# RWKV attention and squared-ReLU FFN on one core: small steps placed by a list scheduler, fixed tiles and PSUM banks, and DMA transposes for 16 of 24 chunks

## The chip, the cores and the metric

The kernel runs on one NeuronCore of a Trainium2 chip. The time is device microseconds from start to end of the program; lower is better. The profile's span (first to last instruction) is about 2 us shorter than the time. Engines: PE is TensorE (PEld its weight loads), DVE is VectorE, ACT is ScalarE, POOL is GpSimd, SP is SyncE, which here only issues DMAs. In the traces here each engine works its instructions off in program order, so one that waits holds up all those behind it: PE stood still for 9.0 us before one transpose (below).

## The reference

Two stages. A recurrent attention with decay `w` and a bonus `u`, then an FFN `relu(x W1)^2 W2`.

```python
batch, n_heads, seq, head_dim = 4, 8, 768, 48          # r, k, v
n_tokens, d_model, d_ff = 3072, 384, 2048
for t in range(S):
    cur = einsum('bhd,bhe->bhde', u * k[t], v[t])
    y[t] = einsum('bhd,bhde->bhe', r[t], state + cur)
    state = w * state + einsum('bhd,bhe->bhde', k[t], v[t])
x = y as (3072, 384)
h = maximum(x @ w_in, 0)
out = (h * h) @ w_out                                   # float32
```

## The kernel before

The sequence is cut into 24 chunks (6 pieces of 128 steps, 4 batches). Within a chunk the recurrence becomes matmuls. Each chunk passes these steps (their names return below):

- kh and rt: k and r times powers of w, to bf16 (POOL; DVE for the first two chunks). P0: r times k times u (POOL), summed by `du` and multiplied with v to `dv` (DVE).
- T: eight 128x128 transposes of kh and rt on PE, copied out of PSUM by ACT (rkT). A: eight matmuls; Bm: two masks on DVE. Y and U: the chunk's output and state update. xs: Y plus dv (DVE). X: three transposes of xs on PE, copied by ACT into xT.
- For each pair of chunks, F1: the first layer in eight slices of six matmuls, relu on ACT, square on DVE; F2: the second layer, eight slices of four matmuls, then a copy by ACT and a store.

The order is written by hand: eight slots per period, in each slot a slice of F1 of one pair, of F2 of the pair before, and a piece of attention of the pair after.

```python
psT, psA, psY, psU: one buffer each (psA has 2 banks);  psH: bufs=2;  psO: bufs=1   # all 8 PSUM banks
...
def piece_F1(g, s):
    hp = psH.tile([128, 2, GT], FP32, tag="H")
    ...                                        # 6 matmuls
    nc.scalar.activation(hr, hp, AF.Relu)
    nc.vector.tensor_mul(hq, hr, hr)           # square, SBUF to SBUF, bf16
...
prep(0, nc.vector); prep_du(0, nc.gpsimd); prep(1, nc.vector); prep_du(1, nc.gpsimd)
for s in range(NS): load_w1(s)                 # 8 DMAs issued by POOL
for s in range(NS): load_w2(s)                 # 8 more
def period(ga, g1, g2):
    for s in range(8):
        if g1 is not None: piece_F1(g1, s)
        if g2 is not None: piece_F2(g2, s)
        if ga is not None:
            att(ga, s)                         # s=0: cast v, T, du/dv; 1: A, T; 2: A, du/dv; 3,4: Y, U; 5,6: X
            ...
            preps(ga + 1, s)                   # POOL, one pair ahead
```

Of the kernel before, what the change touches and what calls it, by code (L numbers as in the profile page):

```python
# [8 lines left out]
FP32 = mybir.dt.float32  # L10
BF16 = mybir.dt.bfloat16
AF = mybir.ActivationFunctionType
ALU = mybir.AluOpType


@with_exitstack
def kernel(
# [19 lines left out]
    HD = H * D  # L37
# [10 lines left out]
    loads = ctx.enter_context(tc.tile_pool(name="loads", bufs=7))  # L48
    work = ctx.enter_context(tc.tile_pool(name="work", bufs=3))
    hid = ctx.enter_context(tc.tile_pool(name="hid", bufs=3))  # L50

    psT = ctx.enter_context(tc.tile_pool(name="psT", bufs=1, space=bass.MemoryType.PSUM))
    psA = ctx.enter_context(tc.tile_pool(name="psA", bufs=1, space=bass.MemoryType.PSUM))
    psY = ctx.enter_context(tc.tile_pool(name="psY", bufs=1, space=bass.MemoryType.PSUM))
    psU = ctx.enter_context(tc.tile_pool(name="psU", bufs=1, space=bass.MemoryType.PSUM))
    psH = ctx.enter_context(tc.tile_pool(name="psH", bufs=2, space=bass.MemoryType.PSUM))
    psO = ctx.enter_context(tc.tile_pool(name="psO", bufs=1, space=bass.MemoryType.PSUM))

    def bcast_rows(src):
        return bass.AP(  # L60
            tensor=src.tensor, offset=src.offset, ap=[[0, 128], list(src.ap[0]), list(src.ap[1])]
        )


    r_v = r.rearrange("b h (c t) d -> b c t h d", t=L)
    k_v = k.rearrange("b h (c t) d -> b c t h d", t=L)
    v_v = v.rearrange("b h (c t) d -> b c t h d", t=L)
    out_v = out.rearrange("(n t) o -> n t o", t=L)
    w_in_t = moe_w_in.rearrange("(c p) f -> p c f", p=128)
    w_out_t = moe_w_out.rearrange("(f p) o -> p f o", p=128)  # L70

    nat = {}

    def load(i):
        if i >= N:
            return
        c, b = i // B, i % B
        rf = loads.tile([128, H, D], FP32, name=f"rf_{i}", tag="rf")
        kf = loads.tile([128, H, D], FP32, name=f"kf_{i}", tag="kf")
        vf = loads.tile([128, H, D], FP32, name=f"vf_{i}", tag="vf")  # L80
        nc.sync.dma_start(out=rf, in_=r_v[b, c])
        nc.sync.dma_start(out=kf, in_=k_v[b, c])
        nc.sync.dma_start(out=vf, in_=v_v[b, c])  # L83
        nat[i] = (rf, kf, vf)

    W1, W2 = [], []

    def load_w1(s):
        t = const.tile([128, CCH, GT], BF16, name=f"W1_{s}")
        nc.gpsimd.dma_start(out=t, in_=w_in_t[:, :, GT * s : GT * (s + 1)])  # L90
        W1.append(t)

    def load_w2(s):
        t = const.tile([128, 2, d_model], BF16, name=f"W2_{s}")
        nc.gpsimd.dma_start(out=t, in_=w_out_t[:, 2 * s : 2 * s + 2, :])
        W2.append(t)
# [4 lines left out]
    nc.sync.dma_start(out=wb, in_=bcast_rows(w))  # L101
    load(0)
    ub = const.tile([128, H, D], FP32, name="ub")
    nc.sync.dma_start(out=ub, in_=bcast_rows(u))
    for i in range(1, 4):
        load(i)
    load(4)
    load(5)

# [4 lines left out]
    nc.gpsimd.iota(njcol_i, pattern=[[0, 1]], base=L - 1, channel_multiplier=-1)  # L114
    identity = const.tile([128, 128], BF16, name="identity")
# [16 lines left out]
    )  # L132

    tcol = const.tile([128, 1], FP32, name="tcol")
    nc.vector.tensor_copy(tcol, tcol_i)
    njcol = const.tile([128, 1], FP32, name="njcol")
    nc.vector.tensor_copy(njcol, njcol_i)
    NB = 4
    rt_buf, kh_buf = [], []
    for j in range(NB):  # L140
        tr = const.tile([128, H, DP], BF16, name=f"rt_{j}")
        tk = const.tile([128, H, DP], BF16, name=f"kh_{j}")
        nc.vector.memset(tr[:, :, D:DP], 0.0)
        nc.vector.memset(tk[:, :, D:DP], 0.0)
        rt_buf.append(tr)
        kh_buf.append(tk)
    wrow = const.tile([1, 2, HP, 128], FP32, name="wrow")
    nc.vector.memset(wrow, 0.0)
    esel = const.tile([1, 2, 2 * D], FP32, name="esel")
    nc.vector.memset(esel, 0.0)  # L150
    nc.vector.memset(esel[:, 0, 0:D], 1.0)
    nc.vector.memset(esel[:, 1, D : 2 * D], 1.0)

    logw = const.tile([128, H, D], FP32, name="logw")
    nc.scalar.activation(logw, wb, AF.Ln)
    Wkhat = const.tile([128, H, D], FP32, name="Wkhat")
    nc.scalar.activation(Wkhat, logw, AF.Exp, scale=njcol)
    Wt2 = const.tile([128, H, D], FP32, name="Wt2")
    nc.scalar.activation(Wt2, logw, AF.Exp, scale=tcol)
    logw_p = logw.rearrange("p (a e) d -> p e a d", e=2)  # L160
    for e in range(2):
        nc.scalar.activation(  # L162
            wrow[:, e, :, 64 * e : 64 * e + D], logw_p[0:1, e], AF.Exp, scale=float(L)
        )

    WLm = const.tile([128, HP, 2 * D], FP32, name="WLm")
    wl_ps = psU.tile([128, HP, 2 * D], FP32, name="wl_ps", tag="U", padded_shape=[None, None, 128])
    for hc in range(HP):
        for e in range(2):
            nc.tensor.matmul(  # L170
                wl_ps[:, hc, :],
                wrow[:, e, hc, :],
                esel[:, e, :],
                start=(e == 0),
                stop=(e == 1),
                skip_group_check=True,
            )
    nc.scalar.copy(WLm, wl_ps)

    S0W = [const.tile([128, HP, 2 * D], BF16, name=f"S0W_{b}") for b in range(B)]  # L180


    du_in, vbs, dvs, rkTs, Bms, xss, xTs = {}, {}, {}, {}, {}, {}, {}

    def prep(i, eng):
        rf, kf, vf = nat[i]
        eng.tensor_mul(kh_buf[i % NB][:, :, 0:D], kf, Wkhat)  # L187
        eng.tensor_mul(rt_buf[i % NB][:, :, 0:D], rf, Wt2)

    def prep_du(i, eng):  # L190
        rf, kf, vf = nat[i]
        P0 = work.tile([128, H, D], FP32, name=f"P0_{i}", tag="P0")
        eng.tensor_mul(P0, rf, kf)  # L193
        eng.tensor_mul(P0, P0, ub)  # L194
        du_in[i] = P0

    def cast_v(i):
        vb = work.tile([128, H, D], BF16, name=f"vb_{i}", tag="vb")
        nc.scalar.copy(vb, nat[i][2])
        vbs[i] = vb  # L200

    def bonus(i):
        P0 = du_in.pop(i)
        du = work.tile([128, H], FP32, name=f"du_{i}", tag="du")
        nc.vector.tensor_reduce(du, P0, axis=mybir.AxisListType.X, op=ALU.add)  # L205
        dv = work.tile([128, H, D], FP32, name=f"dv_{i}", tag="dv")
        du_b = bass.AP(
            tensor=du.tensor, offset=du.offset, ap=[list(du.ap[0]), list(du.ap[1]), [0, D]]
        )
        nc.vector.tensor_mul(dv, nat[i][2], du_b)  # L210
        dvs[i] = dv

    def piece_T(i):
        pt = psT.tile([128, 2, HP, 128], BF16, name=f"pt_{i}", tag="T")
        for j, src in ((1, kh_buf[i % NB]), (0, rt_buf[i % NB])):
            for hc in range(HP):
                nc.tensor.transpose(  # L217
                    pt[:, j, hc, :],
                    src[:, 2 * hc : 2 * hc + 2, :].rearrange("p a b -> p (a b)"),
                    identity,  # L220
                )
        rkT = work.tile([128, 2, HP, 128], BF16, name=f"rkT_{i}", tag="rkT")
        nc.scalar.copy(rkT, pt)  # L223
        rkTs[i] = rkT

    def piece_A(i):
        rkT = rkTs[i]
        Ap = psA.tile([128, 2, HP, 128], FP32, name=f"Ap_{i}", tag="A")
        Bm = work.tile([128, 2, HP, 128], BF16, name=f"Bm_{i}", tag="Bm")
        for hc in range(HP):  # L230
            for e in range(2):
                p0 = 64 * e
                nc.tensor.matmul(
                    Ap[:, e, hc, :],
                    rkT[p0 : p0 + D, 1, hc, :],
                    rkT[p0 : p0 + D, 0, hc, :],
                    start=True,
                    stop=True,
                    skip_group_check=True,
                )  # L240
        for e in range(2):
            nc.vector.tensor_mul(Bm[:, e], Ap[:, e], mask_b)
        Bms[i] = Bm

    def piece_YU(i):
        c, b = i // B, i % B
        rkT, Bm, vb = rkTs.pop(i), Bms.pop(i), vbs.pop(i)
        Y = psY.tile([128, HP, 2 * D], FP32, name=f"Y_{i}", tag="Y", padded_shape=[None, None, 128])
        for hc in range(HP):
            if c > 0:  # L250
                nc.tensor.matmul(
                    Y[:, hc, :], rkT[:, 0, hc, :], S0W[b][:, hc, :],
                    start=True, stop=False, skip_group_check=True,
                )
# [175 lines left out]
```

## Time and profile before

| | before |
|---|---|
| time, median of 3 runs | 221.29 us (220.57 to 221.61) |
| span of the profiled run | 219.5 us |
| PE, DVE, ACT, POOL busy | 81%, 70%, 53%, 60% of the span |

From the first page of the profile, the busy shares. Section 1 gives busy time; section 2 cuts the span in 40 slices of 5.5 us, a digit being the busy share in tenths.

```profile
PE 177.5 (81%) x1784; PEld 131.4 (60%) x1784; DVE 154.1 (70%) x254; ACT 115.8 (53%) x199; POOL 131.5 (60%) x134
PE   0854117587998998998989989989989879999973
DVE  3486006799979889699699798896996993753300
POOL 2597469995396594892993975947929980000000
DMA  5999999996129148075092190391750010010111
```

PE is poorly used in the first nine slices (0 to 49 us), where the DMA line reads 9 for most of the time, and nearly full afterwards. The table of busy time by window has the same in numbers (columns: stretch, its length, busy us and instruction count of PE, PEld, DVE, ACT and POOL, granted PE clock, share of DMA time, GB/s). The share adds up the times of all packets over 16 engines; it reads 1.20 in one stretch here, so it serves to compare stretches and is not a fraction of what the DMA could do:

```profile
0.00:21.30 21.30, 9.39 (x79) 7.71 (x80) 12.45 (x30) 7.71 (x13) 13.85 (x24) 1.00 0.96 168
21.30:49.30 28.00, 14.33 (x127) 9.90 (x127) 13.48 (x21) 9.07 (x16) 22.56 (x24) 1.00 1.20 185
49.30:185.00 135.70, 124.62 (x1335) 93.47 (x1333) 116.08 (x179) 82.99 (x143) 95.14 (x87) 1.00 0.42 92
```

What PE waits for in the first 50 us, from the table of waits (total us, times, longest):

```profile
PE pt_369 L217 <- POOL kh_153 L187: 9.0, 1, 9.0
PE wl_ps L170 <- ACT wrow L162: 6.4, 1, 6.4
```

PE waits 9.0 us for POOL to prepare chunk 2 (kh). POOL is late since it issues sixteen weight loads first, from 12.9 to 30.7 us; from the tenth on it waits 0.5 to 0.9 us before each one for an earlier weight load to land. The DMA view shows what the weight loads do to the loads of r, k and v (KB each, us from issue to landing): 4.4 us without them, 17.8 us beside them.

```profile
kf_91<-in_k_dram SPq DMA_DIRECT2D x1, 192.0 KB, 4.4
...
rf_122<-in_r_dram SPq DMA_DIRECT2D x1, 192.0 KB, 17.8
```

From 64 us on the chain of waits repeats every 15.13 us (63.62 to 78.75). One period of it (start, us, what):

```profile
63.62 0.60 ACT hr_0_841 L310
...
65.21 0.55 DVE du_863 L205
...
66.56 1.14 DVE hq_1_878 L312
67.69 1.20 DVE Bm_885 L242 x2
68.89 0.62 DVE hq_2_916 L312
...
72.49 0.48 DVE xs_979 L272
...
73.01 0.20 PE Y_1000 L251
...
78.06 0.67 PE hp_0_1099 L301 x6
78.75 0.60 ACT hr_0_1106 L310
```

The chain runs through relu, then eight microseconds of DVE in its program order, then Y on PE, then about six microseconds of PE in its program order, and relu again. The step from DVE to PE is the single buffer of Y: Y_1000 starts at 73.01 us, just after xs_979 has read the Y before it out of that buffer.

### The profile page before, as it was taken

Reading aid. Unit: us, or ns where it says so; the run is one execution under the profiler, and the core shown is the slowest. Engines: PE = TensorE matmul, PEld = TensorE weight load, DVE = VectorE, ACT = ScalarE, POOL = GpSimd, SP = SyncE. Lnnn points to the kernel's source line nnn. Section 1 sums busy time; section 2 is a strip of 40 time slices with the busy share of each in tenths; the row PEclk is TensorE's granted clock in tenths of the full one; section 3 lists DMA queues with packets and bytes.
Section 4 is the critical chain, followed back from the end, with each engine's and each line's share of the span. In section 5 each row is a group of like instructions: output and inputs, shape, how many; then the busy total and the mean of one; then the engine's idle time right before and its main releaser. Section 6 shows DMA issues by size and latency. Waiting matters only on the chain.

```text
span 219.5 us, 4540 instructions
## 1 busy us (share of the span) xinstructions
PE 177.5 (81%) x1784; PEld 131.4 (60%) x1784; DVE 154.1 (70%) x254; ACT 115.8 (53%) x199; POOL 131.5 (60%) x134
## 2 busy tenths in 40 slices
PE   0854117587998998998989989989989879999973
PEld 0733015375776776766767757767667657777741
DVE  3486006799979889699699798896996993753300
ACT  4341104466486476583764864765846737745520
POOL 2597469995396594892993975947929980000000
PEclk9999999999999999999999999999999999999999
DMA  5999999996129148075092190391750010010111
GB/s 113 194 186 178 174 182 185 184 200 131 37 56 200 39 104 172 14 162 129 1 214 75 50 206 36 73 184 37 157 130 3 36 39 36 0 39 36 39 52 56
DMA packets 84020, 22.70 MB, mean 103 GB/s; under 512 B 75552, under 2 KB 84000, under 8 KB 84000
## 3 DMA queue, kind: packets, MB, share of 16 engines
q1 hardware_dynamic: 78624, 19.27, 41.8%
q0 software_dynamic: 5376, 3.15, 9.8%
q8 instruction: 14, 0.23, 0.5%
q14 instruction: 6, 0.05, 0.1%
HBM read 20.84 MB, written 4.72 MB: 116 GB/s over the span
## 4 chain that ended last, share of the span: by engine, by line
PE 37%; DVE 34%; issue 8%; DMA 7%; POOL 6%; ACT 4%; SPq 2%; POOLq 0%; ACTq 0%
DMA W_6_211<-in_moe_w_in_dram 5%; DMA kf_99<-in_k_dram 2%; PE o_3289 L323 1%; PE o_3269 L323 1%; PE o_3216 L323 1%; PE o_3152 L323 1%; PE o_730 L323 1%; SPq L83 1%; PE o_3062 L323 1%; PE o_2055 L323 1%; PE o_1790 L323 1%; PE o_995 L323 1%; PE o_2830 L323 1%; PE o_2585 L323 1%; PE o_1260 L323 1%
## 5 line engine op out<-in xcount | busy, mean ns | idle before, releaser
L301 PEld LDWEIGHTS <-W_0_199 128*128 128x128 bf16 x72 | 7.3, 102 | 2.9 <-issue 0.7
L170 PE MATMUL wl_ps<-esel,wrow 1*128 1x96 f32 x16 | 3.7, 423 | 6.4 <-ACT wrow L162 6.4
L205 DVE TENSOR_REDUCE du_380<-P_2_291 128x8 f32<-128x384 f32 x1 | 0.6, 554 | 10.9 <-POOL P_2_291 L194 10.9
L217 PEld LDWEIGHTS <-kh_153 128*128 128x128 bf16 x24 | 1.9, 103 | 10.2 <-POOL kh_153 L187 9.5
L217 PE MATMUL pt_369<-identity,kh_153 128*128 128x128 bf16 x4 | 0.6, 307 | 9.0 <-POOL kh_153 L187 9.0
L301 PEld LDWEIGHTS <-W_3_205 128*128 128x128 bf16 x72 | 6.3, 100 | 2.1 <-issue 0.2
L301 PEld LDWEIGHTS <-W_1_201 128*128 128x128 bf16 x72 | 6.9, 102 | 0.9
L301 PEld LDWEIGHTS <-W_2_203 128*128 128x128 bf16 x72 | 6.9, 102 | 0.9
L170 PEld LDWEIGHTS wl_ps<-esel,wrow 1*128 1x128 f32 x16 | 3.5, 326 | 6.4 <-ACT wrow L162 6.4
L301 PEld LDWEIGHTS <-W_6_211 128*128 128x128 bf16 x72 | 6.6, 98 | 0.7
L301 PEld LDWEIGHTS <-W_7_213 128*128 128x128 bf16 x72 | 6.6, 98 | 0.7
L301 PEld LDWEIGHTS <-W_5_209 128*128 128x128 bf16 x72 | 6.4, 98 | 0.7
L301 PEld LDWEIGHTS <-W_4_207 128*128 128x128 bf16 x72 | 6.4, 97 | 0.7
L223 ACT COPY rkT_378<-pt_369 128x1024 bf16<-128x1024 bf16 x1 | 1.0, 1012 | 9.6 <-PE pt_369 L217 9.6
L280 POOL TENSOR_TENSOR S0W_185<-ts_716,WLm 128x384 bf16<-128x384 f32 x1 | 1.0, 1040 | 5.8 <-DVE ts_716 L279 5.8
L193 POOL TENSOR_TENSOR P_0_191<-rf_90,kf_91 128x384 f32<-128x384 f32 x1 | 1.4, 1372 | 4.1 <-DMA kf_91<-in_k_dram 4.1
L280 POOL TENSOR_TENSOR S0W_185<-ts_1776,WLm 128x384 bf16<-128x384 f32 x1 | 1.1, 1110 | 3.9 <-DVE ts_1776 L279 3.9
L280 POOL TENSOR_TENSOR S0W_187<-ts_981,WLm 128x384 bf16<-128x384 f32 x1 | 1.1, 1109 | 3.9 <-DVE ts_981 L279 3.9
L280 POOL TENSOR_TENSOR S0W_185<-ts_1246,WLm 128x384 bf16<-128x384 f32 x1 | 1.1, 1109 | 3.9 <-DVE ts_1246 L279 3.9
L280 POOL TENSOR_TENSOR S0W_187<-ts_1511,WLm 128x384 bf16<-128x384 f32 x1 | 1.1, 1109 | 3.9 <-DVE ts_1511 L279 3.9
L280 POOL TENSOR_TENSOR S0W_187<-ts_2041,WLm 128x384 bf16<-128x384 f32 x1 | 1.1, 1109 | 3.9 <-DVE ts_2041 L279 3.9
L280 POOL TENSOR_TENSOR S0W_185<-ts_2306,WLm 128x384 bf16<-128x384 f32 x1 | 1.1, 1109 | 3.9 <-DVE ts_2306 L279 3.9
(1198 smaller groups left out, 735.0 us busy)
## 6 DMA issues: line engine op xcount, KB each, us to landing
wb<-in_w_dram SPq DMA_DIRECT2D x1, 192.0 KB, 3.6
rf_90<-in_r_dram SPq DMA_DIRECT2D x1, 192.0 KB, 4.1
kf_91<-in_k_dram SPq DMA_DIRECT2D x1, 192.0 KB, 4.4
vf_92<-in_v_dram SPq DMA_DIRECT2D x1, 192.0 KB, 4.4
ub<-in_u_dram SPq DMA_DIRECT2D x1, 192.0 KB, 4.4
rf_98<-in_r_dram SPq DMA_DIRECT2D x1, 192.0 KB, 4.4
kf_99<-in_k_dram SPq DMA_DIRECT2D x1, 192.0 KB, 4.7
vf_100<-in_v_dram SPq DMA_DIRECT2D x1, 192.0 KB, 4.8
```

Source lines behind the costliest of these rows:

```text
L83: nc.sync.dma_start(out=vf, in_=v_v[b, c])
L170: nc.tensor.matmul(wl_ps[:, hc, :], wrow[:, e, hc, :], esel[:, e, :], start=(e == 0), stop=(e == 1), skip_group_check=True,)
L193: eng.tensor_mul(P0, rf, kf)
L205: nc.vector.tensor_reduce(du, P0, axis=mybir.AxisListType.X, op=ALU.add)
L217: nc.tensor.transpose(pt[:, j, hc, :], src[:, 2 * hc : 2 * hc + 2, :].rearrange("p a b -> p (a b)"), identity,)
L223: nc.scalar.copy(rkT, pt)
L280: nc.gpsimd.tensor_mul(S0W[b], ts, WLm)
L301: nc.tensor.matmul(hp[:, fi, :], W1[s][:, c, 128 * fi : 128 * (fi + 1)], xT[:, c, :], start=(c == 0), stop=(c == CCH - 1), skip_group_chec ...
L323: nc.tensor.matmul(ops[i], hsq[g, f // 2][:, f % 2, L * j : L * (j + 1)], W2[f // 2][:, f % 2, :], start=(f == 0), stop=(f == FCH - 1), sk ...
```

## The change

Intent: keep PE always supplied. The program is cut into some 900 small steps with a duration, an engine, what they depend on, and the buffers and banks they take and free. A list scheduler inside the kernel (it runs when the program is built) simulates the engines and two DMA queues and fixes the order and every buffer. Along with it:

- DMA transposes replace PE's T and X for chunks 8 to 23 (`nT=8, nX=8`);
- half of the squares go to ACT, the other half are taken on DVE as PSUM times relu;
- the weight loads wait (a "gate") until v of chunk 2 has landed; from chunk 2 on, r/k/v come for two chunks per DMA; weights in eight loads of double size;
- WLm (the decay table) is built by POOL instead of sixteen fp32 matmuls; kh/rt of chunks 0 to 7 go to DVE;
- PSUM: three banks shared by all attention steps, three for F1, two for F2.

The core of the diff, cut (`...`):

```diff
+class Step: ...
+def order_steps(steps, pools, sw_rate=0.75, hw_rate=0.17): ...
+PLAN = dict(per=6.2, loads=[...], nprep=8, p1set=2, nT=8, nX=8, gates=[('v', 2), ('v', 2)],
+            sq=(1, 3, 5, 7), ldlead=26, lead=-1, f1lag=0.5, f2lag=8, relup=-3, sqp=-2)
+POOLS = dict(ldr=2, ..., rkT=6, bank=3, bankH=3, bankO=2, Bm=3, xs=3, xT=2, hr=6, hq=28, os=3, ts=2)
...
-        nc.gpsimd.dma_start(out=t, in_=w_in_t[:, :, GT * s : GT * (s + 1)])
+        s_g = st(f"gate{part}", "POOL", 0.1, [Ld[x, i]], prio=-102, emit=go)
+            Ws.append(st(f"W{part}{s}", "POOL", 0.78, [s_g], prio=..., dma=2.32, emit=go))
...
+    def f_XB(i):
+            nc.sync.dma_start_transpose(out=rkTb[...], in_=rk[...].rearrange("p a h d -> p (a h d)"))
+    def f_xX(i):
+            nc.sync.dma_start_transpose(out=xTb[...][:, :, L * (i % 2) : L * (i % 2 + 1)], in_=xsb[...])
...
-        nc.vector.tensor_mul(hq, hr, hr)
+            if eng == "ACT":
+                nc.scalar.activation(hq, hr, AF.Square)
+            else:
+                nc.vector.tensor_mul(hq, hp, hr)        # hp is the PSUM bank
...
+    order, given = order_steps(steps, POOLS)
+    for s in order:
+        s.emit()
```

## The prediction

> **What bounds the kernel now**, by the table of busy time by window, the timeline and the chain of waits:
>
> - 0 to 49.3 us: start-up. PE is busy 23.7 us, 3.7 of them in fp32 matmuls for WLm. The DMA engines are full (168 to 185 GB/s). Sixteen weight loads, issued by POOL from 12.9 us, slow the r/k/v loads: landing takes 4.4 us before and up to 17.8 us beside them. POOL, issuing in order against a full ring, cannot prepare chunk 2 until 30.7 us; PE, in order too, waits 9.0 us for that (table of waits).
> - 49.3 to 185 us: a pattern with a period of 15.13 us per pair of chunks. From the timeline's starts, PE's work in it is: first layer 8 x 0.655, second layer 8 x 0.65, A 2 x 0.36, Y 2 x 0.37, U 2 x 0.17, transposes 2 x (0.44 + 0.17): 13.5 us. About 1.6 us are stalls, and the chain runs half of each period through DVE: masks (0.68 each, two per chunk) and squares, which take 0.42 us alone but 1.1 to 1.2 beside POOL's work.
> - After 185 us: nearly pure PE work, then 3.8 us of tail.
>
> **What the change does**
>
> 1. Transposes of 16 of 24 units leave PE: 1.22 us per pair. PE's work falls to 12.3 us per pair and about 152 us in all. Their copies (1.01 and 0.48 us per chunk) leave ACT.
> 2. Half of the squares go to ACT; the others read PSUM, and I estimate 0.69 us from the mask, equal in size and also from PSUM. DVE falls from 12.9 to about 10 us per pair; ACT stays near 9.2, POOL at 11.2. So PE remains the bound, with POOL close behind.
> 3. The order is finer; PSUM has three attention, three first-layer and two output banks: most of the 1.6 us should go. My period: 12.6 to 13 us.
> 4. Weights start only after the first four chunks' loads (near 18 us), so POOL and PE have work meanwhile; WLm's fp32 matmuls go. The first 45 us stay limited by DMA: the weights need about 25 us while sharing. I expect PE to idle about 21 us before it saturates.
> 5. Added: 32 DMA transposes, of 256 KB and 96 KB. No run shows their duration yet. The Trainium skill, "DMA: Bandwidth & Descriptors", section "Latency and other measured facts", gives 261 GB/s; my estimate from it is 1.0 and 0.4 us. Per pair the DMA then has loads 6.2, stores 1.1 and transposes 2.8: about 10 of 12.7 us.
>
> **Sum** (estimate): 152 PE work + 21 start-up idle + 4 stalls + 4 tail = 181 us; the measured time lies near the span (221.3 against 219.5). Predicted 181, range 171 to 196. Faster by over 2%: 0.96; within 2%: 0.02; slower: 0.02.
>
> **What would show it.** Step 1: PE's busy time down by over 10 us. Steps 2, 3: period near 12.7, PE above 95% busy from about 45 us on, DVE near 78%. Step 4: the first first-layer matmul near 22 us, without a 9 us PE wait after it. Step 5: transposes landing within 4 us, no PE wait on them.
>
> **What would make it wrong.** Transposes much slower than estimated, holding up loads and stores in the one SP queue; loads starving behind weights, so that the fixed PE order stalls at chunks 4 to 7; POOL slowed by DVE's port use to over 12.7 us per pair.

## The result, and the profile after

| | before | after |
|---|---|---|
| time, median | 221.26 us (4 runs) | 183.05 us (182.37 to 184.16, 4 runs) |
| ratio of fast runs | | 0.8285 (95%: 0.8252 to 0.8318) |
| span | 219.5 us | 180.6 us |
| PE, DVE, ACT, POOL busy | 81, 70, 53, 60% | 89, 71, 65, 59% |

Ratios here and below are the mean time of a kernel's fast runs over that of the kernel before in the same rounds, so not quite the ratio of the medians.

The page of the changed kernel, the same lines:

```profile
PE 160.6 (89%) x1592; PEld 118.2 (65%) x1592; DVE 128.6 (71%) x216; ACT 117.5 (65%) x214; POOL 106.8 (59%) x116
PE   0344769899999999999999999999999999999991
DVE  3399998997388838959979696778777889631310
POOL 2346998024940999599879977986968980000000
DMA  3999999999949649979799799897896255221102
```

From slice 9 on (a slice is 4.5 us here) PE is at 9 to the end. And DMA, which had been idle half of the time after 50 us, is now mostly at 7 to 9 tenths up to 140 us. By window:

```profile
0.00:22.00 22.00, 9.00 (x86) 5.84 (x86) 15.78 (x35) 9.08 (x15) 11.18 (x23) 1.00 0.94 180
22.00:45.00 23.00, 20.00 (x217) 16.00 (x216) 20.33 (x35) 16.37 (x29) 11.96 (x13) 1.00 1.23 194
100.00:120.00 20.00, 20.00 (x208) 14.43 (x206) 14.54 (x25) 13.58 (x26) 17.12 (x18) 1.00 0.94 182
```

What PE waits for in the whole run:

```profile
PE bank L429 <- DVE rk L382: 10.2, 4, 6.3
PE bank L454 <- ACT rkT L436: 2.2, 2, 1.1
PE bank L536 <- DVE xs L506: 1.9, 3, 0.8
```

L429 is T, L454 is A, L536 is X: all of them belong to the start. After 38 us the table of waits has 0.6 us in all. The new DMAs (x count, us to landing):

```profile
rkT<-rk SPq DMA_TRANSPOSE x16, 3.4
xT<-xs SPq DMA_TRANSPOSE x16, 3.8
```

**Where the time came from.** Busy PE is a poor measure of work, because matmuls overlap (an F1 matmul lasts 273 ns, yet the next one starts 109 ns after it) and run slower in the start-up (417 to 421 ns, 213 ns apart). How long they run slower differs too: the first record of a full clock is at 40.0 us in the kernel before, at 29.6 us in `before_gate` and at 28.2 us in the changed kernel, so a part of what counts below as lost in the start-up is PE running slower, and not standing still. I count instead the matmuls of each kind in a stretch and price them at their start-to-start times at full speed (F1 0.655 us per six, F2 0.65 per four, T 0.44 per eight, A 0.36, Y 0.37, U 0.17, X 0.17 per step). This is my own arithmetic on counts from the trace. `before_gate` and `before_three` are experiments explained below.

| useful PE work, us | before | before_gate | before_three | after |
|---|---|---|---|---|
| 0 to 49.3 us | 12.2 | 16.6 | 17.2 | 25.3 |
| 49.3 to 100 us | 44.8 | 44.6 | 47.1 | 49.6 |
| 100 to 140 us | 36.2 | 35.8 | 37.6 | 39.7 |
| whole run | 160.6 | 160.6 | 153.5 | 150.9 |
| span minus work | 58.9 | 54.1 | 47.7 | 29.7 |

So the span fell by 38.9 us: 9.7 us because PE has less to do, 29.2 us because it loses less time. Of these 29.2, 13.1 come from the first 49.3 us and 16.1 from later.

### The profile page after: what moved, and what is told of

It reads as the page before. It is cut to its first block, busy times and chain, and to the rows that moved or that the text cites. A ratio compares the mean times of both kernels' runs of the same rounds, so it can differ in the third digit from the quotient of the medians.

```text
span 180.6 us, 4082 instructions
## 1 busy us (share of the span) xinstructions
PE 160.6 (89%) x1592; PEld 118.2 (65%) x1592; DVE 128.6 (71%) x216; ACT 117.5 (65%) x214; POOL 106.8 (59%) x116
## 4 chain that ended last, share of the span: by engine, by line
PE 79%; DVE 9%; DMA 4%; ACT 2%; SPq 2%; issue 1%; DVEq 0%
PE bank L638 34%; PE bank L604 32%; PE bank L454 4%; PE bank L483 3%; DMA ub<-in_u_dram 2%; DMA xT<-xs 2%; PE bank L478 2%; PE bank L429 2%; DVE rk L382 2%; SPq L351 2%; DVE xs L506 2%; DVE dv L411 2%; PE bank L495 2%; DVE Bm L467 1%; ACT rkT L436 1%
## 5 line engine op out<-in xcount | busy, mean ns | idle before, releaser
L618 ACT ACTIVATE hr<-bank 128x512 bf16<-128x512 f32 x96 | 55.9, 595 | 29.4 <-PE bank L604 27.6
L604 PE MATMUL bank<-xT,W 128*128 128x256 bf16 x576 | 73.8, 273 | 0.4 <-DVE hq L629 0.3
L638 PE MATMUL bank<-W,hq 128*128 128x384 bf16 x384 | 72.0, 326 | 0.0
L604 PEld LDWEIGHTS <-W 128*128 128x128 bf16 x576 | 55.0, 98 | 11.8 <-issue 0.9
L638 PEld LDWEIGHTS <-hq 128*128 128x128 bf16 x384 | 36.1, 98 | 19.3
L629 DVE TENSOR_TENSOR hq<-bank,hr 128x512 bf16<-128x512 f32 x48 | 32.6, 683 | 17.4 <-ACT hr L618 17.4
L467 DVE TENSOR_TENSOR Bm<-bank,maskJT 128x512 bf16<-128x512 f32 x48 | 31.1, 681 | 8.2 <-PE bank L454 8.1
L388 POOL TENSOR_TENSOR P<-ldr,ldk 128x384 f32<-128x384 f32 x24 | 28.2, 1177 | 9.9 <-DMA ldr<-in_r_dram 9.9
L528 POOL TENSOR_TENSOR S0W<-ts,WLm 128x384 bf16<-128x384 f32 x16 | 16.5, 1031 | 29.1 <-DVE ts L522 28.9
L626 ACT ACTIVATE hq<-hr 128x512 bf16<-128x512 bf16 x48 | 30.2, 630 | 1.1
L397 POOL TENSOR_TENSOR P<-P,ub 128x384 f32<-128x384 f32 x22 | 22.9, 1043 | 1.4
L651 ACT COPY os<-bank 128x384 f32<-128x384 f32 x24 | 11.4, 476 | 12.4 <-PE bank L638 12.1
L429 PE MATMUL bank<-identity,rk 128*128 128x128 bf16 x64 | 7.5, 273 | 10.5 <-DVE rk L382 10.2
L382 POOL TENSOR_TENSOR rk<-ldr,Wt 128x384 bf16<-128x384 f32 x16 | 16.6, 1040 | 0.1
L429 PEld LDWEIGHTS <-rk 128*128 128x128 bf16 x64 | 5.5, 120 | 12.4 <-DVE rk L382 11.5
L454 PE MATMUL bank<-rkT 48*128 48x128 bf16 x192 | 10.6, 233 | 2.5 <-ACT rkT L436 2.2
L483 PE MATMUL bank<-vb,Bm 128*128 128x48 bf16 x192 | 12.2, 189 | 0.4 <-DVE Bm L467 0.4
```

What stands on the lines that cost most here:

```text
L382: e.tensor_mul(rk[slot[f"rk{i}"]][:, j, :, 0:D], ld[x][slot[f"{x}P{i // 2}"]][:, i % 2], tab)
L388: nc.gpsimd.tensor_mul(P0b[slot[f"P0{i}"]], ld["r"][slot[f"rP{i // 2}"]][:, i % 2], ld["k"][slot[f"kP{i // 2}"]][:, i % 2])
L397: (nc.vector if eng == "DVE" else nc.gpsimd).tensor_mul(t, t, ub)
L454: nc.tensor.matmul(heads(f"bA{i}{e}", "bank", 128)[:, hc, :], rkT[p0 : p0 + D, HP + hc, :], rkT[p0 : p0 + D, hc, :], start=True, stop=True ...
L467: nc.vector.tensor_mul(Bmb[slot[f"Bm{i}"]][:, e], heads(f"bA{i}{e}", "bank", 128), mask_b)
L483: nc.tensor.matmul(Y[:, hc, D * e : D * (e + 1)], Bm[:, e, hc, :], vb[:, 2 * hc + e, :], start=(c == 0), stop=True, skip_group_check=True,)
```

## The experiments

Twelve kernels, all with correct results. "before" in their ratios is the kernel before, run in the same rounds. In all_pe, sq_back, no_gate, banks_back and tuned the scheduler computes the order and the buffers anew, so these change along with the edit; xbar_twice, twice_split and warm keep the order.

### 1. All transposes back on PE (all_pe)

```diff
-nT=8, nX=8
+nT=24, nX=24
```

> The changed kernel with all 24 units transposed on TensorE again (nT=24, nX=24); the list scheduler reorders accordingly. Theory A (TensorE is saturated from about 38 us on, so its work adds one to one): 16 units x 0.61 us = 9.8 us more, 183 to 193 us (190 to 196), PE busy near 100% in 60 to 140 us as before, and 16 rkT copies (1.01 us) and 16 xT copies (0.48 us) back on ACT, 24 us in all, which still fit. Rival B (the gain is the order and the banks; the DMA transposes only move work to a DMA queue that is itself nearly full): at most 186 us.

Measured: 191.61 us (191.5 to 191.72), ratio 0.867. That is 8.6 us above the changed kernel; 9.8 were expected. Its PE work counts 160.8 us, and span minus work is 28.9 us, about the same as with DMA transposes (29.7). The two kernels over 80 to 140 us, first all_pe:

```profile
80.00:140.00 60.00, 60.00 (x661) 46.11 (x658) 46.25 (x74) 48.70 (x88) 48.98 (x48) 1.00 0.57 126
```

and the changed kernel:

```profile
80.00:140.00 60.00, 59.65 (x623) 44.47 (x620) 49.02 (x79) 42.60 (x79) 50.55 (x50) 1.00 0.92 189
```

PE is full in both. Theory A holds: with PE saturated, work taken off it counts nearly one to one. The price is on the DMA, whose share rises from 0.57 to 0.92.

### 2. Squares back on DVE (sq_back)

```diff
-sq=(1, 3, 5, 7)
+sq=()
-                nc.vector.tensor_mul(hq, hp, hr)
+                nc.vector.tensor_mul(hq, hr, hr)
```

> The changed kernel with all 96 squares on VectorE from SBUF as in the kernel before (hr*hr), nothing on ACT. Theory A: VectorE gets 48 squares more and each lasts 0.42 to 1.2 us beside POOL's work; its busy time goes from 129 us to about 180 us, so VectorE becomes the bound: 200 us (192 to 212). Rival B (VectorE had room, squares do not matter once the order is fine): at most 187 us.

Measured: 195.52 us (194.11 to 196.6), ratio 0.8842. Theory A holds. The 96 squares last 770 ns on average (683 ns for the 48 that read PSUM in the changed kernel). DVE is full from 60 to 100 us (39.3 of 40 us), but PE loses little there. The losses lie in 40 to 60 and 100 to 160 us: there the counted work of PE is 67.2 us of 80, against 78.7 in the changed kernel, and DVE is busy 75.3 us. One of these stretches, and PE's wait for DVE's masks over the whole run:

```profile
140.00:160.00 20.00, 18.10 (x184) 13.18 (x185) 19.96 (x31) 8.84 (x17) 15.81 (x15) 1.00 0.68 131
PE bank L454 <- DVE Bm L467: 3.8, 5, 2.2
```

Total DVE busy was 161 us, not 180: the squares were slowed less than I had taken from the kernel before. With this plan, the split of the squares is needed for PE to be the bound.

### 3. Weight loads without the gate (no_gate)

```diff
-        s_g = st(f"gate{part}", "POOL", 0.1, [Ld[x, i]], prio=-102, emit=go)
-            Ws.append(st(f"W{part}{s}", "POOL", 0.78, [s_g], ...
+            Ws.append(st(f"W{part}{s}", "POOL", 0.78, [], ...
```

> The changed kernel with the gate before the weight loads taken away, so that POOL issues all eight at about 2 us. Theory A (r/k/v loads starve beside weight loads): the loads of chunks 0 and 1 land only when the weights do (about 25 us), the first first-layer matmul comes after 35 us instead of 27.4 us, total 190 to 200 us. Rival B (the same bytes have to come in anyway, so only their order changes): 181 to 185 us.

Measured: 193.84 us (192.76 to 193.91), ratio 0.8759; the first F1 starts at 36.8 us instead of 27.5. The loads of v for chunks 0 and 1 took 14.3 us to land, against 4.5 us:

```profile
ldv<-in_v_dram SPq DMA_DIRECT2D x2, 192.0 KB, 14.3
```

The same bytes in another order cost 10.8 us. Theory A holds.

### 4. The kernel before with the squares split (before_sq)

```diff
-        nc.vector.tensor_mul(hq, hr, hr)
+        if s % 2:
+            nc.scalar.activation(hq, hr, AF.Square)
+        else:
+            nc.vector.tensor_mul(hq, hp, hr)
```

> The kernel before with one part of the change: odd squares on ACT, even ones on VectorE reading PSUM. Theory A (half of each 15.13 us period runs through VectorE, squares being the stretched part): the period falls towards TensorE's 13.5 us, to about 14.1 us; some 10 periods, so 221 to about 211 us (206 to 216). Rival B (the stalls come from the coarse order and the single banks, not from the squares): over 218 us.

Measured: 218.41 us (217.59 to 218.91), ratio 0.9878. Theory A fell. DVE went down to 47.8 of 80 us (60 to 140 us), yet the period only went from 15.13 to 14.59 us (79.86 to 94.45 in its chain). The chain now runs through ACT, where relu, square and the rkT copy stand in one order, and then as before through DVE and PE. Relieving the engine in the chain did not free PE; the loop closed through the next one.

### 5. The kernel before with later weight loads (before_gate)

```diff
-    for s in range(NS): load_w1(s)
-    for s in range(NS): load_w2(s)
 ...
                 preps(ga + 1, s)
+                if ga == 0 and s == 7:
+                    for t in range(NS): load_w1(t)
+                    for t in range(NS): load_w2(t)
```

> The kernel before with only the weight loads issued later: POOL issues the sixteen after it has prepared chunks 2 and 3 (about 22 us instead of 12.9 us). Theory A (weights crowd out the r/k/v loads, and POOL stands against a full ring): chunks 2 and 3 are prepared by about 22 us instead of 38 us, the saturated part starts some 6 us earlier, 221 to about 215 us (211 to 218). Rival B (start-up is limited by the sum of bytes, so their order does not matter): 219 to 223 us.

Measured: 216.86 us (216.39 to 217.34), ratio 0.983. Theory A holds in direction and range; the 9 us wait for POOL is gone, but a new wait of 5.3 us stands in the table: F1 for its first weights. The work done by 49.3 us rises from 12.2 to 16.6 us, a third of the 13.1 that the changed kernel gains there. Its period stays 15.14 us (89.11 to 104.25 in its chain).

### 6. The kernel before with k/r transposes on the DMA (before_xbar)

```diff
+    xb = ctx.enter_context(tc.tile_pool(name="xb", bufs=5))
+    def cross_T(i):
+        rkT = xb.tile([128, 2, HP, 128], BF16, tag="rkX")
+        for j, src in ((1, kh_buf[i % NB]), (0, rt_buf[i % NB])):
+            nc.sync.dma_start_transpose(out=rkT[:, j], in_=src.rearrange("p h d -> p (h d)"))
+        rkTs[i] = rkT
     def piece_T(i):
+        if i >= 8:
+            return
 ...  cross_T(i) right after prep(i), for i >= 8
```

> The kernel before with only the k/r transposes of chunks 8 to 23 moved to the DMA crossbar, issued one period ahead right after their preparation (the xs transposes stay on TensorE). TensorE's work falls by 0.88 us per pair, 7 us in all; ACT loses 16 copies of 1.01 us. Theory A (in the kernel before a chain through VectorE and ACT sets the period, not TensorE's work): the gain is less than half of that, 217.5 to 220 us. Rival B (TensorE is the bound there too, with constant stalls): 7 us or more, at most 214.5 us.

Measured: 220.30 us (219.67 to 220.7), ratio 0.9976: nothing within the 95% interval (0.9951 to 1.0001). Theory A expected a little more. Its chain shows why; the period is 15.13 us to the last digit although PE has 0.88 us less to do in it:

```profile
79.44 0.61 ACT hr L319
...
94.57 0.61 ACT hr L319
```

The transposes are not in the loop. PE, in the kernel before, is busy but not the bound: the loop through ACT, DVE and PE is.

### 7. Each DMA transpose twice (xbar_twice)

```diff
+    spareB = [const.tile([128, 2 * HP, 128], BF16, ...) for j in range(4)]
+    spareX = [const.tile([128, CCH, L], BF16, ...) for j in range(4)]
             nc.sync.dma_start_transpose(out=rkTb[...], in_=rk[...])
+            nc.sync.dma_start_transpose(out=spareB[i % 4], in_=rk[...])
             nc.sync.dma_start_transpose(out=xTb[...], in_=xsb[...])
+            nc.sync.dma_start_transpose(out=spareX[i % 4], in_=xsb[...])
```

> The changed kernel with each of the 32 DMA transposes issued twice, the second into spare tiles nobody reads (result stays right). Theory A (the prediction: DMA used 10 of 12.7 us per pair, so a second set of 2.8 us just about fits): at most 187 us. Theory B (the SP queue is the thin spot: in 60 to 140 us SP spends 72 to 95% of the time in issuing, a transpose holding it 1.2 us and more): 4.9 us more issue time per pair than about 11 us, so a period of about 16 us instead of 12.3 for 8 pairs: 195 to 215 us.

Measured: 215.58 us (214.94 to 215.8), ratio 0.976, just above theory B's range. All but 5 us of the change's gain is gone. PE now waits for the transposes:

```profile
PE bank L459 <- DMA rkT<-rk: 19.0, 8, 3.9
PE bank L612 <- DMA xT<-xs: 3.6, 3, 1.7
```

A second set costs 32.5 us over 16 chunks, 4.1 us a pair, where the prediction had 2.8 us of DMA time and room for it. Adding up SP's issue entries in the timeline, SP is occupied 85 to 89% of 80 to 140 us in the changed kernel and 94 to 95% here. That is an upper bound on issuing, for an entry contains waiting too: the second copies, which wait for no other engine, hold SP for 1.25 us (X) and 1.33 us (k/r) in the median, the first ones for up to 2.9 us, and in the start-up of the changed kernel two plain loads hold it for 6.1 and 9.4 us beside the weight loads. The DMA share is 0.85 here, lower than the changed kernel's 0.92. Part of the loss is indirect: PE's clock. The trace has five stretches of half clock, of 3.41 us or twice that and 23.9 us together, all between 84 and 174 us; each begins in or within about 1 us of a wait of PE for a transpose, of 2.1 to 3.9 us. In one of them twelve F1 matmuls take 2.72 us, against 1.31 us at full clock. So up to 12 us of the 32.5 (an estimate, half of the 23.9) is PE running at half speed, and not DMA time.

### 8. The same with the stores issued by ACT (twice_split)

```diff
-            nc.sync.dma_start(out=out_v[...], in_=osb[...])
+            nc.scalar.dma_start(out=out_v[...], in_=osb[...])
```

> The run with doubled DMA transposes (215.6 us), with the 24 stores of the output issued by ACT instead of SP. Theory A (SP's issuing is what ran out: a pair takes about 16 us of it, the stores 1 to 3 us of that): 8 pairs shorter by 1 to 2.5 us, 196 to 208 us. Rival B (the DMA engines ran out, whoever issues): 213 to 217 us.

Measured: 212.90 us (210.22 to 213.79; the last counts as slow), ratio 0.9586: neither range, just below rival B's 213. SP's entries still fill 93 to 95% of the time, but much of that is waiting: between 80 and 140 us the first copy of an X transpose takes 2.4 us in the median, the second mostly 1.25 us. The DMA share of 80 to 140 us rises from 0.85 to 0.93, where the changed kernel has 0.92. Neither number shows a limit reached. What ends first, SP's issuing, the DMA engines, or the waits in SP's order between them, stays open.

### 9. PE kept busy in the start-up (warm)

```diff
+    def warm(n):
+        for _ in range(n):
+            nc.tensor.matmul(banks[7][:, 0:128], identity, identity, start=True, stop=True, ...)
+    warm(36)                       # before anything else on PE
 ...                               # warm(6) after each of the first 12 PE steps and inside the first four T
```

> The changed kernel with TensorE kept busy in the start-up: 36 matmuls of identity by identity into an unused bank before the first transposes, 6 after each of the first 12 TensorE steps and between the two halves of the first four k/r transposes. Theory A (the first 29 us run at half speed, 128x256 matmuls 421 ns instead of 273 ns, because TensorE had been idle; its steps are part of the start-up chain): early matmuls near 273 ns and 178 to 182 us. Theory B (start-up is bound by DMA and VectorE, TensorE's speed does not show): 182 to 184 us, though the matmuls are faster.

Measured: 183.15 us (183.08 to 183.16 in three of four runs, 185.3 in one), ratio 0.8319: theory B. The trace shows how far the attempt went (start, us, engine, line, tiles; L293 is the added matmuls):

```profile
1.68 4.02 PE L293 MATMUL bank<-identity 128*128 128x128 bf16 x36 [1.68 <-POOL identity masks.py:199]
...
13.91 0.79 PE L293 MATMUL bank<-identity 128*128 128x128 bf16 x6
14.52 0.35 PE L503 MATMUL bank<-vb,rk 128*128 128x96 bf16 x4
14.70 0.50 PE L293 MATMUL bank<-identity 128*128 128x128 bf16 x6
```

The six added matmuls take 0.79 to 0.85 us until 14 us (107 ns from start to start) and 0.50 us afterwards (56 ns), so PE reached full speed at 14.5 us, where the changed kernel reaches it at 28.2 us. Yet the first F1 starts at 26.98 us instead of 27.48, and nothing is left of that at the end. So PE's speed is not what the start-up waits for. What it does wait for is not settled by this run: DVE is the busier engine in the changed kernel (15.8 of the first 22 us, 20.3 of the next 23), and the chain of warm runs through DVE from 9.0 to 17.3 us, but then 13.7 us through one load of v, which lands at 31.6 us beside the weights (27.2 us in the changed kernel) and holds up ACT with the relus behind it.

### 10. Three parts of the change together, in the old order (before_three)

Experiments 4, 5 and 6 in one kernel, nothing else:

```diff
+        rkT = xb.tile(...)  ... nc.sync.dma_start_transpose(...)     # as in before_xbar
-        nc.vector.tensor_mul(hq, hr, hr)
+        if s % 2: nc.scalar.activation(hq, hr, AF.Square)            # as in before_sq
+        else:     nc.vector.tensor_mul(hq, hp, hr)
-    for s in range(NS): load_w1(s)                                   # both moved to the end of
-    for s in range(NS): load_w2(s)                                   # the first period, as in before_gate
```

> The kernel before with three parts of the change at once (later weight loads, squares half on ACT and half from PSUM, k/r transposes of chunks 8 to 23 on the DMA), but its coarse pieces, its order and its PSUM banks kept. Apart they gave -4.0, -2.4 and -0.5 us. Theory A (what is left, the loop through in-order engines, single attention banks and one output bank, still sets a period above TensorE's 12.6 us): 209 to 215 us; the period may come down to about 14. Rival B (the three parts are the gain once they act together): at most 195 us.

Measured: 202.79 us (202.45 to 203.48), ratio 0.9174. Neither range: my theory A was too low on the parts acting together. Apart they gave 2.4, 4.0 and 0.5 us, 7 in all; together they give 18.5. The period is 13.44 us (99.84 to 113.28 in its chain), and most of that chain is now PE itself. What remains in each period is PE's wait for the single output bank, and ACT's order before it:

```profile
97.35 0.61 ACT hr L319
98.00 0.52 issue
98.52 0.47 ACT os L346
99.03 0.81 PE o L335 x4
```

The gate's part of this left the period at 15.14 us when alone, so the shorter period most likely comes from squares and transposes together; that pair was not run.

The last 20 us to the changed kernel lie in what these three parts leave out: the new order, the banks, the other transposes (X), the early preparation, the larger loads, WLm without PE and more buffers. Of these only the division of the banks was tried apart (next experiment).

### 11. Banks divided as before (banks_back)

```diff
-bank=3, bankH=3, bankO=2
+bank=5, bankH=2, bankO=1
```

> The changed kernel with the PSUM banks divided as in the kernel before: two for the first layer and one for the output (five instead of three for attention); the list scheduler reorders accordingly. Theory A (a first-layer bank is held through relu and, for half of them, the square, 0.6 + 0.69 us, and one output bank makes TensorE wait for each copy of 0.48 us): TensorE stalls again, 186 to 192 us. Rival B (the finer order alone does it, banks do not matter): at most 184.5 us.

Measured: 187.16 us median of four, fast runs 185.78 to 187.25 (one run of 191.66 us counts as slow), ratio 0.843. Theory A holds, for 3 us by the ratio. Work done by 49.3 us is 23.3 us (25.3 with the new division), 38.3 in 100 to 140 us (39.7), and at the end PE waits 0.57 us for the one output bank. The five attention banks stay shared by all steps here, while the kernel before gave T, Y and U one buffer each and A two banks. So this run does not test the single Y buffer that stands in the old loop.

### 12. Five numbers of the plan (tuned)

```diff
-per=6.2, p1set=2, f1lag=0.5, f2lag=8, relup=-3
+per=5.8, p1set=3, f1lag=0,   f2lag=9, relup=-4
```

> The changed kernel with five numbers of its plan changed (pace 5.8 instead of 6.2, relu and first layer earlier, second layer later, one more u-product on VectorE), meant to shorten the start-up. Theory A (only the start-up, 25.5 us of lost TensorE time, has anything left to give): 180 to 182.5 us. Rival B (start-up is held by DMA and VectorE, priorities do not help): 182.5 to 185 us.

Measured, six runs: 179.47, 180.89, 181.05 and 181.86 us fast, 182.24 us counted as slow, and the profiled run, 220.03 us. Ratio of the fast runs 0.8176 (0.8143 to 0.8210), so this version is faster than both kernels, by 1.3% against the changed one (0.8176 / 0.8285). The total lies in theory A's range. The run of 182.24 us is called slow only for being over 1.5% above the fastest; its clock was full (0.998), and with it the mean is 181.1 us. The profiled run says nothing about the order; its clock line (tenths of full speed) shows the reason:

```profile
PEclk9999987777777777777777777777777777777777
```

Whether those 2 us were saved in the start-up, as theory A has it, was not seen.

## Why the prediction was right or wrong

181 us were predicted and 183.05 measured (span 180.6). The sum held, though two of its terms were off in opposite directions, and one step of its argument was wrong. That it came within half a microsecond of the span is in part luck: start-up was 3 us too little, stalls 2 us too much, and PE's work and the tail another 1.5 us too much.

- **PE's work, 152 us:** right. Counted from the trace it is 150.9 us. Putting the transposes back costs 8.6 us where 9.8 were reckoned (all_pe).
- **Start-up idle, 21 us:** too small. PE does 25.3 us of work in the first 49.3 us, so 24.0 us are lost. "The first first-layer matmul near 22 us" came at 27.5 us. The prediction names only the DMA and the weights here and does not price the early attention steps. In the trace the first weights land at about 25 us, DVE is busy 20.3 of the 23 us from 22 to 45 us, and PE's early matmuls take 417 ns instead of 273. Which of these held the first F1 back stays open: in warm a faster PE brought it only 0.5 us forward.
- **Stalls, 4 us:** too large. From 49.3 us to PE's last matmul at 177.0 us, 2 us are lost (131.3 us of span minus 125.7 of work minus 3.6 of tail). The 3 us too little of the start-up and these 2 us too much nearly cancelled.
- **Tail, 4 us:** right, 3.6 us.
- **"13.5 us. About 1.6 us are stalls", and "So PE remains the bound":** this step was wrong for the kernel before. It treated the 15.13 us as PE's 13.5 us plus 1.6 us of stalls. before_xbar took 0.88 us of PE's work out of each period and the period stayed 15.13 us; before_sq took DVE down to 60% and gained 0.54 us. The period was set by a loop through in-order engines, ACT, DVE and PE, and none of the three parts that were tried alone opens it. Together they do: 13.44 us with three parts (before_three), and with order and banks PE does 39.7 us of work in 40. The prediction came out right since it priced the end state, in which PE really is the bound, and not each step from the old one.
- **Period (step 3):** right. Loads of k are issued every 12.1 to 12.8 us in the steady part, where 12.6 to 13 were predicted, and PE is busy 131.6 of the 132 us from 45 to 177 us ("above 95%").
- **Squares (step 2):** right in the 0.69 us for those that read PSUM (683 ns measured), and DVE at 78% was predicted where 49.0 of 60 us (82%) are measured over 80 to 140 us. sq_back shows that this term is needed: DVE full in the stretches where PE loses time, 195.5 us.
- **Weights after the first loads (step 4):** right. Without the gate it is 10.8 us slower.
- **DMA transposes (step 5):** right for the change: they land after 3.4 and 3.8 us in the median (longest 4.4 and 4.8), where 4 us were foreseen, and no PE wait on them stands among the waits. The estimated transfer times and the "about 10 of 12.7 us" of DMA time were not tested, since no trace shows a bare transfer and the DMA share is no fraction of a capacity. What failed is the room that they seemed to leave: a second set costs 4.1 us a pair, a part of it through PE's clock. The change fits; a second set does not.

What stays open: what ends first when the transposes are doubled, SP's issuing, the DMA engines or the waits in SP's order (twice_split fell between the theories); how the last 20 us between before_three and the changed kernel divide (some 3 of them are the new division of the banks; order, early preparation on DVE, the remaining transposes, larger loads and buffers were not tried apart); and why one run of tuned had a clock of 0.785.

## What to carry to other kernels

When an in-order program repeats with a fixed period and no engine is full, look for the loop that the chain of waits closes, and judge a change by whether it opens that loop: three edits worth 2.4, 4.0 and 0.5 us alone gave 18.5 us together. Once one engine is saturated, every microsecond of work taken from it counts nearly in full, and it pays to move that work to something that looks idle, here the DMA; but check the new carrier's issuing engine as well as its bytes, since doubling the moved work cost 32.5 us, and these runs do not show which of the two set that price. In a start-up limited by DMA, put the loads that feed the first dependent work ahead of the bulk loads: the same bytes in the other order cost 10.8 us.

## What the Trainium skill lacked or had wrong

- "DMA: Bandwidth & Descriptors", section "Issuing engines are not separate DMA queues": it says that issuing from several engines only saves the sequencer's time to initiate a DMA, "which is usually small relative to the DMA itself". For these SBUF-to-SBUF transposes it was not small: each entry held SP at least 1.2 us (median 1.47 us for 256 KB, 1.20 us for 96 KB, up to 2.6, waiting included), of 3.4 and 3.8 us until landing. The page gives no such time in microseconds for this chip; its only times for it are sequencer cycles of "previous generations".
- The same page, section "Latency and other measured facts": 261 GB/s for DMA transposes led to an estimate of 1.0 and 0.4 us. No trace shows the bare transfer time. But landing took 3.4 and 3.8 us in the median (3.0 and 2.3 at the least), and doubling all transposes cost 4.1 us per pair against the estimated 2.8, a part of it through PE's clock. A bandwidth alone was not enough to price them.
- "TensorE: Matmul & The Clock Gate", section "Part 1: The HAM clock gate (the "warmup" mystery)": it gives about 3.4 us of sustained activity until full speed, in a window that runs freely. In the run warm, 36 matmuls back to back for 4.02 us did not bring full speed (a burst of that length need not fill a free-running window, so this does not contradict the page), and the steady but broken work after them brought it only at 14.5 us, 12.8 us after the first matmul. What broken work does to the clock is what the page lacks. The profile's clock column does not show it: it reads 1.00 in the start-up, although the trace holds no clock record before 40.0 us (before), 28.2 us (changed) and 14.5 us (warm). The slow early matmuls are only seen in their durations (in the changed kernel 417 ns against 273 ns for 128x256).
- The same page, section "Seeing it yourself", has a limiter with a clock of 13/16 and says that one or two busy cores never trip it. One of six runs of tuned, a program on a single core, ran at a granted clock of about 0.75 from 30 us on (0.785 as the mean) and took 220.03 us instead of about 181. What the chip's other cores did at that time is not known here, so this does not contradict the page; but 0.75 is not 13/16 either.
